# Unread products ahead of MLP1, strided products one place sooner, and one local tile behind the second score round, in a sparse-attention and MLP kernel

## The chip, the cores and the metric

The kernel runs on one core of a Trainium2 chip. The metric is the device time of one execution in microseconds (us), median of several. A profile is a look at one execution, and its span is some 1.8 us shorter than the device time of the same execution. TensorE does the matmuls, VectorE (DVE) and ScalarE (ACT) the elementwise work, GpSimd (POOL) casts and masks, and the SyncE queue (SPq) issues most transfers.

## The reference, cut to what matters

Eight batches of 576 tokens go through attention with eight heads. Four heads are local (a token sees the 32 last tokens), four strided (it sees earlier tokens of the same residue modulo 32). The result, 4608 x 512, goes through an MLP.

```python
x = attn_out.transpose(0, 2, 1, 3).reshape(B * S, H * D)   # 4608 x 512
h = x @ w_in                                               # 512 -> 2048   (MLP1)
g = h * np.tanh(np.log1p(np.exp(h)))
return g @ w_out                                           # 2048 -> 512   (MLP2)
```

## The kernel before: the parts that matter

The MLP works in nine blocks `t` of 512 tokens. The attention of batch `t + 1` is cut into steps that are issued between the groups of four matmuls of block `t`: `str_steps` (strided products with v, one step behind each item of MLP1) and `loc_steps` (local scores and products, and the next batch's strided scores, behind the items of MLP2). Scores go through ScalarE (exponential), a mask on VectorE or GpSimd, and the product with v on TensorE (`V`). VectorE then divides by the sums and transposes (`xt_str`). PSUM tiles of the products rotate over two buffers.

```python
def str_steps(b):
    ...
    return [
        [], [], [V(0)], [V(1)], [V(2)], [V(3)], [V(4)], [V(5)], [V(6)], [V(7), a.xt_str],
    ]

def loc_steps(b, x, y):
    ...
    return [
        [],
        [Q(x, ("l", 0)), Q(None, ("l", 2), *n2), Q(y, ("l", 1)), M("l", 0), M("l", 2)],
        [], [],
        [V(0), V(1), M("l", 1)],
        [V(5)] + ([Q(x, ("n", 0)), Q(y, ("n", 1))] + N) * more + [a.xt_str_copy],
        ...
```

Ahead of the first block, batch 0 is worked off alone, and TensorE waits often:

```python
a.pv2("l", 0, 1)
a.mask("l", 2, Dv)
a.pv2("l", 2, 0)
a.pv("l", 4)       # gap behind it: the mask of the last scores
a.pv("l", 5)       # gap behind it: VectorE's divisions
a.xt("l", 0)
a.xt("l", 1)
...                # then MLP1 of block 0
```

The softmax here doesn't subtract the row's maximum and nothing guards it: scores larger than these inputs give would overflow.

## Time and profile before

| | before |
|---|---|
| device time, first three runs | 314.27 us (314.21 to 314.87) |
| span of the profile | 312.8 us |
| TensorE busy | 94% |
| MLP1's first matmuls at half speed | 7 |
| stalls of TensorE at local products (near 150, 183, 213 us) | 0.57, 0.23, 0.25 us |

A stall here is the start of a group less the start of the group before it and the time of its matmuls (0.216 us for 512 columns). The profile's own bracket is shorter (0.40 us near 150 us, against 0.57), since the ends of matmuls in it are modelled. The lines stand in the prediction below.

### The profile page before, as it was taken

Reading aid. Unit: us, or ns where it says so; the run is one execution under the profiler, and the core shown is the slowest. Engines: PE = TensorE matmul, PEld = TensorE weight load, DVE = VectorE, ACT = ScalarE, POOL = GpSimd, SP = SyncE. Lnnn points to the kernel's source line nnn. Section 1 sums busy time; section 2 is a strip of 40 time slices with the busy share of each in tenths; the row PEclk is TensorE's granted clock in tenths of the full one; section 3 lists DMA queues with packets and bytes.
Section 4 is the critical chain, followed back from the end, with each engine's and each line's share of the span. In section 5 each row is a group of like instructions: output and inputs, shape, how many; then the busy total and the mean of one; then the engine's idle time right before and its main releaser. Section 6 shows DMA issues by size and latency. Waiting matters only on the chain.

```text
span 312.8 us, 5771 instructions
## 1 busy us (share of the span) xinstructions
PE 295.3 (94%) x2376; PEld 156.2 (50%) x2376; DVE 164.6 (53%) x378; ACT 182.6 (58%) x195; POOL 102.4 (33%) x109
## 2 busy tenths in 40 slices
PE   0687999999999999999999999999999999999995
PEld 0563455544454445554469754545454444444444
DVE  7673066700571048569786988698869870000000
ACT  1673653476647673867786778677767937215501
POOL 9199043263046105230791079108800000000000
PEclk9999999999999999999999999999999999999999
DMA  6999999999999999999987999898330030011011
GB/s 174 203 226 206 221 185 199 176 168 130 222 188 207 126 221 187 197 165 211 188 162 127 208 169 185 146 198 159 103 107 2 0 132 4 0 67 69 0 67 67
DMA packets 96985, 45.14 MB, mean 144 GB/s; under 512 B 79040, under 2 KB 89600, under 8 KB 96960
## 3 DMA queue, kind: packets, MB, share of 16 engines
q1 hardware_dynamic: 85520, 35.66, 61.8%
q0 software_dynamic: 11152, 8.92, 18.8%
q8 instruction: 18, 0.29, 0.4%
q10 hardware_dynamic: 288, 0.21, 0.2%
q14 instruction: 7, 0.06, 0.1%
HBM read 36.78 MB, written 9.44 MB: 148 GB/s over the span
## 4 chain that ended last, share of the span: by engine, by line
PE 85%; DVE 11%; ACT 2%; issue 1%; DVEq 0%
PE psh L507 38%; PE pso L530 31%; PE po L323 5%; PE pso L557 4%; PE ps L286 3%; DVE xs_t L397 3%; DVE Pl L307 2%; DVE ks L149 1%; DVE x_l L335 1%; PE trx L362 1%; PE tr L209 1%; DVE x_s L335 1%; PE trx L372 1%; DVE rden L334 1%; DVE Ps L601 0%
## 5 line engine op out<-in xcount | busy, mean ns | idle before, releaser
L507 PE MATMUL psh<-xT,w_in 128*128 128x512 bf16 (+1 forms) x640 | 131.9, 361 | 0.3 <-ACT Ps L299 0.3
L530 PE MATMUL pso<-w_out,gT 128*128 128x512 bf16 x512 | 121.8, 379 | 0.0
L513 ACT ACTIVATE gT<-psh 128x1024 bf16<-128x1024 f32 x72 | 72.4, 1023 | 50.1 <-PE psh L507 50.1
L507 PEld LDWEIGHTS <-w_in 128*128 128x128 bf16 x640 | 60.5, 98 | 57.1 <-issue 2.5
L530 PEld LDWEIGHTS <-gT 128*128 128x128 bf16 x512 | 45.4, 98 | 45.8
L149 POOL CAST kl<-kl 96x768 bf16<-96x768 f32 (+1 forms) x13 | 12.5, 984 | 78.8 <-DMA kl<-in_k_dram 78.8
L397 DVE STREAM_TRANSPOSE xs_t<-x_s 32x512 bf16<-32x512 bf16 x48 | 33.7, 702 | 0.9
L334 DVE RECIPROCAL rden<-po 72x4 f32<-72x4 f32 (+1 forms) x100 | 17.6, 176 | 28.1 <-PE po L323 27.2
L537 ACT COPY osb<-pso 128x1024 f32<-128x1024 f32 x16 | 17.6, 1100 | 24.3 <-PE pso L530 13.9
L307 DVE TENSOR_TENSOR Ps<-Ps,consts_sb 72x864 bf16<-72x864 bf16 (+3 forms) x15 | 10.2, 688 | 38.6 <-ACT Ps L299 38.6
L149 DVE COPY osb<-pso 128x512 f32<-128x512 f32 (+1 forms) x2 | 1.1, 558 | 51.3 <-PE pso L557 51.3
L388 DVE STREAM_TRANSPOSE xT<-x_l 32x384 bf16<-32x384 bf16 x48 | 27.3, 569 | 0.7
L149 POOL CAST vl<-vl 128x768 bf16<-128x768 f32 (+2 forms) x30 | 23.6, 785 | 9.0 <-DMA vl<-in_v_dram 7.6
L299 ACT ACTIVATE Ps<-ps 72x864 bf16<-72x864 f32 (+3 forms) x21 | 17.4, 860 | 13.4 <-PE ps L286 13.4
L335 DVE TENSOR_TENSOR x_s<-po,rden 72x256 bf16<-72x256 f32 x56 | 23.5, 420 | 1.9
L323 PEld LDWEIGHTS <-Ps 72*128 72x128 bf16 x256 | 15.5, 101 | 12.0 <-DVE Ps L307 0.8
L404 ACT COPY xT<-xs_t 128x576 bf16<-128x576 bf16 x8 | 21.4, 2938 | 0.0
L299 ACT ACTIVATE Pl<-ps 128x960 bf16<-128x960 f32 (+1 forms) x20 | 17.3, 874 | 3.7 <-PE ps L286 3.5
L335 DVE TENSOR_TENSOR x_l<-po,rden 96x256 bf16<-96x256 f32 x44 | 18.5, 421 | 1.5
L323 PE MATMUL po<-vs,Ps 72*128 72x65 bf16 x256 | 18.2, 201 | 0.7 <-DVE x_s L349 0.5
L147 ACT COPY xT<-trx 128x576 bf16<-128x576 bf16 x16 | 9.9, 636 | 14.7 <-PE trx L372 11.5
L149 POOL CAST ql<-ql 96x768 bf16<-96x768 f32 (+1 forms) x13 | 12.2, 965 | 8.7 <-DMA ql<-in_q_dram 8.7
(73 smaller groups left out, 224.3 us busy)
## 6 DMA issues: line engine op xcount, KB each, us to landing
out_dram<-osb SPq DMA_DIRECT2D x16, 512.0 KB, 4.9
vs<-in_v_dram SPq DMA_DIRECT2D x8, 576.0 KB
vl<-in_v_dram SPq DMA_DIRECT2D x8, 576.0 KB, 11.2
kl<-in_k_dram SPq DMA_DIRECT2D x7, 576.0 KB, 17.0
ql<-in_q_dram SPq DMA_DIRECT2D x7, 576.0 KB, 10.8
w_out<-in_moe_w_out_dram POOLq DMA_DIRECT2D x4, 512.0 KB, 14.2
ks<-in_k_dram POOLq DMA_DIRECT2D x7, 288.0 KB, 8.0
qs<-in_q_dram POOLq DMA_DIRECT2D x7, 288.0 KB, 8.8
```

What stands on the lines that cost most here:

```text
L149: eng.tensor_copy(out_, in_)
L299: nc.scalar.activation(pt[0:n, :, 0:nw], t[0:n, :, o0:o0 + nw], AF.Exp, scale=scale)
L323: nc.tensor.matmul(po[:, h, :], lhsT=pt[0:n, c0:c0 + 128], rhs=rhs, start=True, stop=True,)
L334: nc.vector.reciprocal(rden[0:m, :], po[0:m, :, D])
L335: nc.vector.tensor_tensor(out=dst.rearrange("p (h d) -> p h d", h=4), in0=po[0:m, :, 0:D], in1=rden[0:m, :].unsqueeze(2).to_broadcast([m, ...
L388: nc.vector.transpose(dst[32 * q:32 * q + 32, :, :, m:m + 32], src[m:m + 32, :, :, q, :])
L397: nc.vector.transpose(xs_t[32 * q:32 * q + 32, :, :, m:m + 32], src[m:m + 32, :, :, q, :])
L404: nc.scalar.copy(xT[:, 2 + c, t0:t0 + S].rearrange("p (n j) -> p j n", j=CS), xs_t[:, :, c, 0:PN])
L507: nc.tensor.matmul(ps[:, u, o:o + n], lhsT=w_in[:, cc, fc * 128:(fc + 1) * 128], rhs=xT[:, cc, a:a + n], start=(cc == 2 and o == 0), stop= ...
L513: nc.scalar.activation(gT[:, 2 * g:2 * g + 2, :], ps[:], AF.Mish)
L530: nc.tensor.matmul(p[:, ot % 2, :], lhsT=gT[:, fc, 128 * ot:128 * ot + 128], rhs=w_out[:, fc, :], start=(fc == 0), stop=(fc == 15),)
L537: nc.scalar.copy(osb[:], p[:])
```

## The change

Its intent: keep the array busy ahead of MLP1, so that its clock is already at full rate when MLP1 starts (26.55 us before); and let VectorE begin its transposes of the strided outputs sooner, so that the masks of the local scores no longer wait behind them.

```diff
-            [], [], [V(0)], [V(1)], [V(2)], [V(3)], [V(4)], [V(5)], [V(6)], [V(7), a.xt_str],
+            [], [V(0)], [V(1)], [V(2)], [V(3)], [V(4)], [V(5)], [V(6)], [V(7), a.xt_str],
...
-            [V(5)] + ([Q(x, ("n", 0)), Q(y, ("n", 1))] + N) * more + [a.xt_str_copy],
+            ([Q(x, ("n", 0)), Q(y, ("n", 1))] + N) * more + [a.xt_str_copy, V(5)],
...
+    def fill(t, *widths):
+        for w in widths:
+            nc.tensor.matmul(t[:, 0:w], lhsT=ident, rhs=kTs[0][:, 0:w], start=True, stop=True)
...
         a.pv("l", 4)
+        fill(acc(2, "fill")[:, 0, :], 512, 256)
         a.pv("l", 5)
+        fill(acc(2, "fill")[:, 0, :], 512, 512)
```

## The prediction

It puts the fill at 23.55 to 24.19 and 24.45 to 25.30 us: 0.64 us for 768 columns and 0.85 us for 1024. That is an estimate, and the slow matmuls of MLP1 bear it out: their weight loads from 26.97 to 29.53 us stand 0.427 us apart, for 512 columns each.

> **What bounds the kernel now.** I read the page first (who is busy, what the chain of work is made of), then the chain in order of time, then the TensorE timeline at the places where the chain left TensorE, then the timelines of VectorE and the weight loads there. The page:
>
> ```profile
> PE 295.3 (94%) x2376; PEld 156.2 (50%) x2376; DVE 164.6 (53%) x378; ACT 182.6 (58%) x195; POOL 102.4 (33%) x109
> PE 85%; DVE 11%; ACT 2%; issue 1%; DVEq 0%
> ```
>
> TensorE sets the time. [...] VectorE's 11% of the chain counts only where TensorE stood still for it. So I looked for stalls of TensorE, and for matmuls slower than they can be.
>
> First place, the start of MLP1 (TensorE timeline, then weight loads):
>
> ```profile
> 22.25 1.29 PE L323 MATMUL po<-vl,Pl 128*128 128x65 bf16 x20
> 24.16 0.40 PE L323 MATMUL po<-vl,Pl 128*128 128x65 bf16 x4 [0.63 <-DVE Pl L307]
> 25.55 1.21 PE L362 MATMUL trx<-consts_sb,x_l 96*128 96x96 bf16 x12 [0.98 <-DVE x_l L335]
> 26.55 5.75 PE L507 MATMUL psh<-xT,w_in 128*128 128x512 bf16 x19
> ```
>
> ```profile
> 28.68 0.15 PEld L507 LDWEIGHTS <-w_in 128*128 128x128 bf16 x1 [0.28 <-issue]
> 29.11 0.15 PEld L507 LDWEIGHTS <-w_in 128*128 128x128 bf16 x1 [0.28 <-issue]
> 29.53 2.48 PEld L507 LDWEIGHTS <-w_in 128*128 128x128 bf16 x12 [0.28 <-issue]
> ```
>
> Two gaps, of 0.63 and 0.98 us, stand right ahead of MLP1. Then MLP1's weight loads come singly every 0.43 us until 29.53 us, and from there twelve in 2.48 us, 0.21 us each. Later a block of 64 such matmuls takes 13.81 us in the chain, 0.216 us each. So seven matmuls of MLP1 (26.55 to 29.53) ran at half speed. The page's row of granted clock shows full speed in that slice: it doesn't show this, the spacing does.
>
> Second place, the second products in the blocks where scores, masks and products interleave with MLP2 (TensorE, then VectorE, then the chain one block later):
>
> ```profile
> 147.41 2.76 PE L530 MATMUL pso<-w_out,gT 128*128 128x512 bf16 x12
> 150.57 0.43 PE L323 MATMUL po<-vl,Pl 128*128 128x65 bf16 x8 [0.40 <-DVE Pl L307]
> ```
>
> ```profile
> 140.59 8.58 DVE L397 STREAM_TRANSPOSE xs_t<-x_s 32x512 bf16<-32x512 bf16 x12
> 149.20 1.58 DVE L307 TENSOR_TENSOR Pl<-Pl,consts_sb 128x960 bf16<-128x960 bf16 x2
> ```
>
> ```profile
> 180.79 1.55 DVE Pl L307 x2
> 182.34 0.10 DVE rden L334
> ...
> 182.47 0.43 DVE x_l L335
> 182.90 0.05 issue
> 182.94 0.30 PE po L323 x4
> ```
>
> The twelve matmuls from 147.41 are through at 147.41 + 12 x 0.216 = 150.00; the local products start at 150.57. They wait for the mask of the local scores, which stood behind the twelve transposes of the strided outputs on VectorE (140.59 to 149.17).
>
> [...]
>
> **The change part by part.**
>
> *Unread products.* Added: matmuls of 512 and 256 columns in the first gap, 512 and 512 in the second. [...] The first gap opens when the twentieth product ends: the group starts at 22.25, 20 x 0.065 = 1.30, so 23.55. Filled to 24.19, where the next product starts at 24.16 now: 0.03 us late, and nobody feels it, since VectorE is busy until 24.95 with the tiles before. The four products take 0.26, so the second fill lies from 24.45 to 25.30, and the transposes start at 25.55. The fill thus costs the path nothing; no operand of it arrives late, and the accumulator it writes was read last at 22.5.
> What it may save: seven matmuls x (427 - 216) = 1.48 us, and if the array is warm before 25.55, perhaps 0.2 us more in the twelve transposes. [...] I take 60% for the full saving of 1.5 us, 25% for about a third of it, 15% for none: 0.9 + 0.13 = about 1.0 us.
>
> *Strided products one place sooner.* The eight groups of products come behind items 1 to 8 of MLP1 in place of 2 to 9. They are 0.99 us apart, so VectorE starts its transposes 0.99 us sooner and ends at 148.2 instead of 149.17. The mask then needs ScalarE's exponentials, ready at 147.44 + 0.97 = 148.41. It moves from 149.20 to about 148.45, 0.75 us sooner. It took 1.32 us here beside a GpSimd cast (0.65 elsewhere), so it ends by 149.8, ahead of TensorE's 150.00. Stall of this block gone: 150.57 - 150.00 = 0.57. In the block at 212 us the twelve matmuls from 210.09 end at 212.68 and the products start at 212.94: 0.25 us; the mask there moves from 211.94 to about 211.15, enough. The block at 244 us has no such stall.
>
> *One local tile behind the second score round.* Its stall is in the block at 183 us: TensorE was ready at 182.72 (products 181.59, 0.27 for eight, 0.86 for four matmuls) and began at 182.94 when VectorE had emptied the first of the two rotating PSUM tiles: 0.23 us. Now 28 score matmuls (0.56 us) come before it, and the masks come 0.75 us sooner. Either suffices. It also lets the scores start 0.13 us sooner; ScalarE isn't bound there.
>
> Sum of the stalls: 0.57 + 0.25 + 0.23 = 1.05 us, all on TensorE's path. The counts of work stay as they were, but for the four added matmuls. With the fill: 1.05 + 1.0 = about 2.1 us.
>
> **The rivals.**
> 1. *The fill does not release the clock.* [...] Its failure would leave 1.05 us: 313.2.
> 2. *The clock comes early, but a transfer takes the place of the wait.* The transposes by DMA of the strided queries, issued at 67.39, land 9.6 us later at 77.0; their first readers run at 78.9. That queue runs on its own loads, so a TensorE 1.5 to 1.7 us ahead arrives at 77.2 to 77.4, with 0.2 us left. It would eat at most some tenths: 312.3. Against it: it still fits. The weights fit: the small copy that waits for the last part of w_in is issued at 32.77, and that part is first read after 48 matmuls, at 26.55 + 48 x 0.216 = 36.9.
> 3. *VectorE becomes the wait at the start of the strided products.* In the block at 161 us its transposes of local outputs end at 163.31, and the first strided product will now want VectorE at 163.46 instead of 164.46. That leaves 0.15 us; a miss would delay VectorE only, which then has 0.36 us idle per product to catch up. Worth zero, and up to 0.1 us if not. GpSimd's cast of v for that block ended at 162.24, before its first reader at 163.13.
> 4. *The stalls come back later*, at MLP1's accumulators, which ScalarE frees (161.71 to 162.72 for the second). ScalarE's work follows TensorE's, so both move together; I see no new wait.
>
> **Range and chances.** 314.27 - 2.1 = 312.2, and I take 312.1 us, since warm transposes may add a little. With all of the clock gain, 311.4; with none, 313.2; runs scatter by 0.3 to 0.6. The range is 311.2 to 313.4. Two per cent would be 6.3 us, three times all I can find: faster 0.01, same 0.98, slower 0.01.
>
> **What would show it.** Right: MLP1's first weight loads 0.21 us apart from the start; no single ones at 0.43 us. The local products start where the twelve MLP2 matmuls end, in all four blocks. The masks start at the end of the exponentials. Wrong: singles at 0.43 us for 3 us after the fill; a TensorE wait on a transfer near 77 us; the first gap's products later than 24.3 us; or stalls at the local products left.

## The result, and the profile after

| | before | changed |
|---|---|---|
| device time, median of six runs | 314.81 us (314.21 to 316.19) | 312.70 us (312.04 to 313.23) |
| ratio of fast runs | | 0.9924 (0.9897 to 0.9951) |
| span of the profile | 312.8 us | 311.5 us |

A ratio is the mean time of one kernel's fast runs over that of the other's in the same rounds, so it isn't quite the ratio of the medians. The change is worth 0.76%, 2.4 us.

The changed kernel's TensorE timeline at the start of MLP1 (start, duration, what, times, and in brackets the idle time before it and what ended it):

```profile
22.53 1.29 PE L323 MATMUL po<-vl,Pl 128*128 128x65 bf16 x20
24.05 0.42 PE L489 MATMUL fill<-kTs,consts_sb 128*128 128x256 bf16 x1 [0.22 <-issue]
24.45 0.40 PE L323 MATMUL po<-vl,Pl 128*128 128x65 bf16 x4
24.66 0.78 PE L489 MATMUL fill<-kTs,consts_sb 128*128 128x512 bf16 x2
25.83 0.98 PE L362 MATMUL trx<-consts_sb,x_l 96*128 96x96 bf16 x12 [0.39 <-DVE x_l L335]
26.65 7.72 PE L512 MATMUL psh<-xT,w_in 128*128 128x512 bf16 x34
```

and its weight loads there:

```profile
26.38 0.28 PEld L362 LDWEIGHTS <-x_l 96*128 96x128 bf16 x6 [0.28 <-DVE x_l L335]
26.61 7.48 PEld L512 LDWEIGHTS <-w_in 128*128 128x128 bf16 x36
```

The reader is to see 36 weight loads in 7.48 us, 0.21 us each, from the very first: no single loads 0.43 us apart are left. (One record of the first gap's fill is missing from the trace, as some are: it has 2342 matmuls and 2380 weight loads.) The trace records when the granted clock rose: 25.04 us here, 29.54 us before.

The local products, same places as before (TensorE, then VectorE):

```profile
147.02 2.76 PE L535 MATMUL pso<-w_out,gT 128*128 128x512 bf16 x11
149.62 0.42 PE L323 MATMUL po<-vl,Pl 128*128 128x65 bf16 x8
```

```profile
139.34 8.57 DVE L397 STREAM_TRANSPOSE xs_t<-x_s 32x512 bf16<-32x512 bf16 x12
148.06 0.93 DVE L307 TENSOR_TENSOR Pl<-Pl,consts_sb 128x960 bf16<-128x960 bf16 x2
```

The twelve matmuls (eleven on record) from 147.02 are through at 149.61, and the products start at 149.62. The masks end at 148.99, 0.63 us ahead of that. The stalls near 183 and 213 us are gone too (nothing over 0.12 us is left there). So the parts did what they were meant to. But the span fell by 1.3 us only, where 1.5 us at the clock and 1.05 us at the stalls make 2.5. The rest is in two waits that the kernel before did not have. The first, on the TensorE timeline and then on the queue that serves it:

```profile
75.92 1.89 PE L535 MATMUL pso<-w_out,gT 128*128 128x512 bf16 x8
78.70 0.57 PE L286 MATMUL ps<-qTs,kTs 64*128 64x72 bf16 x24 [0.89 <-DMA qTs<-qs]
```

```profile
60.36 8.81 SPq L170 DMA_TRANSPOSE kTs<-ks  x1
69.27 5.98 SPq L170 DMA_TRANSPOSE qTs<-qs  x1
```

The strided queries of batch 2 are transposed by a transfer that was issued at 69.27 here (67.39 before) and landed 9.3 us later. Before, TensorE came at 78.93 and found them. Now it was ready at 77.65, and stood for 1.05 us. The second is in the block near 162 us: 0.17 us ahead of the first strided product. Both are looked at below.

### The profile page after: what moved, and what is told of

Its sections match the earlier page's. It is cut to its first block, busy times and chain, and to the rows that moved or that the text cites.

```text
span 311.5 us, 5741 instructions
## 1 busy us (share of the span) xinstructions
PE 291.6 (94%) x2342; PEld 155.9 (50%) x2380; DVE 162.8 (52%) x378; ACT 182.7 (59%) x195; POOL 102.0 (33%) x109
## 4 chain that ended last, share of the span: by engine, by line
PE 71%; DMA 16%; SPq 7%; DVE 2%; POOL 2%; issue 1%; ACT 0%; POOLq 0%
PE psh L512 30%; PE pso L535 29%; DMA vl<-in_v_dram 9%; PE pso L562 4%; DMA w_in<-in_moe_w_in_dram 4%; PE po L323 4%; DMA qTs<-qs 3%; SPq L170 3%; SPq L120 3%; PE ps L286 3%; POOL vl L149 2%; DVE x_l L335 1%; DVE x_s L335 1%; SPq L581 0%; DVE rden L334 0%
## 5 line engine op out<-in xcount | busy, mean ns | idle before, releaser
L512 PE MATMUL psh<-xT,w_in 128*128 128x512 bf16 (+1 forms) x629 | 129.4, 357 | 0.8 <-ACT Ps L299 0.3
L535 PE MATMUL pso<-w_out,gT 128*128 128x512 bf16 x487 | 117.7, 379 | 1.9 <-issue 0.6
L307 DVE TENSOR_TENSOR Ps<-Ps,consts_sb 72x864 bf16<-72x864 bf16 (+3 forms) x15 | 8.3, 556 | 40.9 <-ACT Ps L299 40.9
L149 POOL CAST ql<-ql 96x768 bf16<-96x768 f32 (+1 forms) x13 | 11.4, 903 | 11.5 <-DMA ql<-in_q_dram 11.5
```

What stands on the lines that cost most here:

```text
L149: eng.tensor_copy(out_, in_)
L512: nc.tensor.matmul(ps[:, u, o:o + n], lhsT=w_in[:, cc, fc * 128:(fc + 1) * 128], rhs=xT[:, cc, a:a + n], start=(cc == 2 and o == 0), stop= ...
L535: nc.tensor.matmul(p[:, ot % 2, :], lhsT=gT[:, fc, 128 * ot:128 * ot + 128], rhs=w_out[:, fc, :], start=(fc == 0), stop=(fc == 15),)
```

## The experiments

Twelve kernels ran, four to a chip, each beside the kernel before on the same chip. Ratios are to the kernel before of the same call; the three calls were on three chips, so absolute times are compared within a call only. The profiled execution is the first of each kernel's runs, and not always a typical one: it was the slowest of the changed kernel's six, of e1's seven, e2's six, e6's five and e11's eighteen. A wait that its profile shows need not be in the median.

**What each profile showed.** The columns: when the clock rose; how many of MLP1's weight loads were spaced 0.43 us and not 0.21; the stall at the queries of batch 2; and the stall ahead of the first strided product of the block near 162 us (in us, only those over 0.12, from the starts of matmuls). "First look" is the changed kernel's profile in the result above; e6 is the second look at the same kernel.

| run | fill | clock rose | half speed | queries | first strided product | span |
|---|---|---|---|---|---|---|
| before | none | 29.54 | 7 | | | 312.8 |
| changed, first look | full | 25.04 | 0 | 1.05 | 0.17 | 311.5 |
| e1, fill only (slow) | full | 25.02 | 0 | 3.71 | | 316.4 |
| e2, moves only | none | 28.64 | 5 | 1.45 | 1.33 | 313.8 |
| e3, strided move only | none | 30.05 | 8 | | | 312.0 |
| e4, late v (wrong) | full | 26.73 | 0 | | | 310.6 |
| e5, late v, mended | full | 26.58 | 0 | | | 310.9 |
| e6, changed again | full | 27.86 | 3 | | 0.48 | 311.3 |
| e7, v cast first | full | 27.00 | 1 | | | 310.2 |
| e8, both mends | full | 25.09 | 0 | | | 310.2 |
| e9, half-height fill | half | 30.47 | 9 | | | 312.1 |
| e10, fill of transposes | full | 25.09 | 0 | | 1.63 | 312.1 |
| e11, second gap only | part | 28.35 | 4 | | 1.93 | 314.3 |
| e12, moves, v cast first | none | 32.01 | 12 | | | 312.7 |

### The parts apart: e1, e2, e3

e1 undoes both moves and keeps the fill. e2 takes the two `fill` lines out. e3 is e2 with the local tile put back:

```diff
-            ([Q(x, ("n", 0)), Q(y, ("n", 1))] + N) * more + [a.xt_str_copy, V(5)],
+            [V(5)] + ([Q(x, ("n", 0)), Q(y, ("n", 1))] + N) * more + [a.xt_str_copy],
```

> Only the unread products; strided and local products where they were before. Theory T1 (the fill releases the clock some 4 us sooner, but TensorE then meets the queries' transfer for batch 2, which lands at about 77 to 78.6 us whatever TensorE does): MLP1 is at full speed from its first weight load, a TensorE wait of 0.3 to 1 us on the queries' transfer stands near 77 us, the three stalls near 150, 183 and 213 us stay, and the time falls by only 0.4 to 1.0 us. Rival R1 (the fill's 1.5 us come out in full): falls by 1.4 to 1.6 us. Rival R2 (the fill gives nothing): within 0.2 us of before.

Measured: 313.36 us against 315.16, ratio 0.9937 (0.9915 to 0.996): 2.0 us less (1.3 to 2.7). That is above the 0.4 to 1.0 us of T1; R1's 1.4 to 1.6 us lie inside the interval. The clock rose at 25.02, as in the changed kernel. The profiled execution was of the slow state, so it is left out of every ratio, but its trace says itself what happened to it (stretch and its length, then the busy time of PE, PEld, DVE, ACT and POOL with their counts of instructions, granted clock, share of the DMA engines, GB/s):

```profile
74.00:77.00 3.00, 3.00 (x16) 1.30 (x14) 0.00 (x0) 2.28 (x3) 0.00 (x0) 1.00 1.56 122
77.00:80.00 3.00, 0.33 (x2) 0.00 (x0) 0.00 (x0) 0.96 (x1) 0.00 (x0) 0.94 1.27 131
80.00:83.00 3.00, 1.79 (x27) 1.23 (x29) 0.60 (x1) 1.55 (x2) 0.00 (x0) 0.50 0.78 153
83.00:86.00 3.00, 3.00 (x16) 1.35 (x15) 1.01 (x3) 0.12 (x1) 0.00 (x0) 0.50 0.95 300
```

TensorE came 3.71 us ahead of the queries' transfer, and the clock fell again: at 79.63, for 6.83 us. Nothing more is concluded from that execution.

> Only the two moves, no unread products. T1: the three stalls of 0.57, 0.23 and 0.25 us vanish, the time falls by about 1.05 us (0.8 to 1.3); MLP1 starts with six to a dozen matmuls at half speed. Rival (stalls come back as others, at the accumulators or behind ScalarE): falls by less than 0.6 us.

Measured: 314.12 us, 0.9975 (0.9948 to 1.0001): 0.8 us less, with an interval from none to 1.6. MLP1 started with five slow matmuls (six to a dozen were expected). All three stalls at the local products were gone in the profile. But it had two new ones: 1.45 us at the queries, with no fill and so no early TensorE (the transfer was simply late in that execution, the slowest of the six), and this (TensorE, then GpSimd):

```profile
161.77 1.91 PE L512 MATMUL psh<-xT,w_in 128*128 128x256 bf16 x16
164.84 0.28 PE L323 MATMUL po<-vs,Ps 72*128 72x65 bf16 x4 [1.17 <-POOL vs L149]
```

```profile
155.05 1.60 POOL L149 CAST ql<-ql 96x768 bf16<-96x768 f32 x2 [2.63 <-DMA ql<-in_q_dram]
156.60 0.72 POOL L102 DMA_DIRECT2D ks<-in_k_dram  x1
157.31 0.71 POOL L102 DMA_DIRECT2D qs<-in_q_dram  x1
158.11 4.85 POOL L307 TENSOR_TENSOR Ps<-Ps,consts_sb 72x1008 bf16<-72x1008 bf16 x3
162.91 1.88 POOL L149 CAST vs<-vs 72x2048 bf16<-72x2048 f32 x1
```

The strided products, now behind the second item of MLP1, read v in bf16, which GpSimd casts last in a queue that starts when q has landed. With q cast from 155.05 (151.72 before), the cast ended at 164.79, and the product waited for it.

> Only the strided products one place sooner. If either move suffices for the stall near 183 us, as the prediction said, the time equals that of both moves (1.05 us below before, within 0.15) and no stall of over 0.1 us is left at the local products. Rival: the local tile's move is needed, a stall of about 0.2 us stays near 183 us and the time is 0.2 to 0.3 us above that of both moves.

Measured: 313.79 us, 0.9959 (0.994 to 0.9978): 1.3 us less. No stall of over 0.1 us at the local products, near 183 us too (the eight products start at 181.33, four matmuls, the fifth tile at 182.45 without a wait). So the local tile's move was not needed once the strided products came sooner; either move would do, as predicted, though the local move alone was not run. That e2 seems slower than e3 is within the two intervals.

### The two waits: e4 to e8

e4 puts the load of batch 2's local v behind that batch's transposes in the same queue; e5 is its mended form; e7 lets GpSimd cast the strided v ahead of the masks; e8 has both; e6 is the changed kernel itself.

```diff
 # e5
-            load_v(2)
+            load_v_str(2)
...
-            cast_v(2, Po, Po)
+            cast(Po, vs[0][0:PN, :, :, 0:D], vs32[0:PN])
...
-                at[9] += [lambda: str_by_dma(2), lambda: loc_by_dma(2)]
+                at[9] += [
+                    lambda: str_by_dma(2), lambda: loc_by_dma(2),
+                    lambda: load_v_loc(2), lambda: cast_v_loc(2, Po),
+                ]
 # e7
-                    at[5].append(lambda: cast_v(t + 2, Po, Po))
+                    at[5].insert(2, lambda: cast(
+                        Po, vs[t % 2][0:PN, :, :, 0:D], vs32[0:PN]
+                    ))
+                    at[5].append(lambda: cast_v_loc(t + 2, Po))
```

> The changed kernel, with the load of the local v of batch 2 (576 KB) behind the transposes by DMA of batch 2 in the same queue, not ahead of them. T1: the queries' transfer lands 2 to 3 us sooner, TensorE no longer waits near 77 us, and the time falls by a further 0.5 to 1.0 us below the changed kernel, to about 2.3 to 2.6 us below before in all. Rival (the wait near 77 us is a chance of one execution): no difference to the changed kernel, 2.0 to 2.2 us below before.

Its result was wrong (relative error 0.20): the cast of the local v stayed ahead of the moved load and took the old batch's values. Its time is not used.

> The run with the late load of v, mended: its cast of the local v moves behind the load too (the first try cast the old batch's v and gave a wrong result). T1: no TensorE wait on the queries' transfer near 78 us, 0.3 to 1.0 us faster than the changed kernel of the same rounds. Rival: equal to the changed kernel within 0.15 us.

> The changed kernel again, in the same rounds as its variants. T1: the clock rises before MLP1's first weight load; a wait of 0.3 to 1.5 us on the queries' transfer near 78 us; the first strided product of the block near 162 us waits 0 to 1.3 us for GpSimd's cast of v; about 312.5 us, 2 us below before. Rival: a profile without these two waits and the same time, so that they cost nothing in most executions.

> The changed kernel, with GpSimd casting the strided v ahead of the masks of the next block's strided scores, not behind them, in the three blocks that do it there. T2 (the strided products, one place sooner, now meet that cast): the cast ends 2 to 3 us before its first reader, no wait on it is left near 162 us, and the time is 0.1 to 0.6 us below the changed kernel. Rival (the wait of the run with the moves only was a chance): equal within 0.15 us; or slower, if v lands later than the cast is now wanted and holds up the masks.

> Both mends: late load of the local v of batch 2, and the strided v cast first. T1 and T2: the gains add; TensorE has no wait of over 0.35 us after MLP1's start but the one for an accumulator near 130 us and the small ones of the second and third block; 0.5 to 1.4 us below the changed kernel, some 311.5 us. Rival: a further transfer takes over and the time stays within 0.3 us of the better single mend.

| run | median | ratio to before (315.46) | 95% interval |
|---|---|---|---|
| e6, changed | 312.35 us | 0.9906 | 0.9889 to 0.9923 |
| e5, late v | 312.74 us | 0.9908 | 0.9889 to 0.9927 |
| e7, v cast first | 312.19 us | 0.9916 | 0.9877 to 0.9956 |
| e8, both | 312.51 us | 0.9905 | 0.9887 to 0.9922 |

(e7's runs hold one of 316.38 among five from 311.82 to 312.39.) In the profiles the mends did what they were to do. In e5 the queries' transfer was issued early:

```profile
58.63 2.65 SPq L170 DMA_TRANSPOSE kTs<-ks  x1
61.34 4.33 SPq L170 DMA_TRANSPOSE qTs<-qs  x1
```

eight microseconds sooner than in the changed kernel's first look, six sooner than in its second, and TensorE found them. In e7 the cast ran from 154.36, and its first reader came at 161.18:

```profile
154.36 1.89 POOL L149 CAST vs<-vs 72x2048 bf16<-72x2048 f32 x1 [0.25 <-DMA vs<-in_v_dram]
156.29 4.83 POOL L307 TENSOR_TENSOR Ps<-Ps,consts_sb 72x1008 bf16<-72x1008 bf16 x3
```

But none of it shows in the times: the four ratios lie between 0.9905 and 0.9916, and I had expected 0.5 to 1.4 us of e8. The intervals would still allow some 0.8 us between e8 and e6. The changed kernel's second look tells why at least in part. On this chip the queries were there in time, with no fix at all, and the wait for the cast was 0.48 us:

```profile
160.08 1.91 PE L512 MATMUL psh<-xT,w_in 128*128 128x256 bf16 x16
162.31 0.28 PE L323 MATMUL po<-vs,Ps 72*128 72x65 bf16 x4 [0.32 <-POOL vs L149]
```

(That look also missed an expectation: the clock rose at 27.86, after MLP1's first loads, and three matmuls ran at half speed.) And the late load of v brought a wait of its own, which e8's expectation of no new wait over 0.35 us missed. GpSimd could cast the local v only from 82.24, and TensorE stood 0.45 us for it (TensorE, then GpSimd):

```profile
86.26 0.29 PE L323 MATMUL po<-vl,Pl 128*128 128x65 bf16 x4 [0.29 <-POOL vl L149]
```

```profile
82.24 3.97 POOL L149 CAST vl<-vl 128x768 bf16<-128x768 f32 x4 [11.75 <-DMA vl<-in_v_dram]
```

In e5 a stall of 0.30 us stands at the same products, with no cause named by its profile; the kernels without the late load have none there.

So the two waits are real where they occur, and hang on when the transfers land in that execution. The eleven looks at kernels that share this queue's order had the queries issued at 67.39 to 69.27 us; in the two looks at the changed kernel it was 69.27 and 67.60. No version is shown to beat the changed kernel.

### What releases the clock: e9 to e12

e9 gives the fill 64 rows in place of 128, e10 makes it of transposes, e11 leaves out the first gap's fill, and e12 is e2 with e7's edit.

```diff
 # e9
-            nc.tensor.matmul(t[:, 0:w], lhsT=ident, rhs=kTs[0][:, 0:w], start=True, stop=True)
+            nc.tensor.matmul(t[:, 0:w], lhsT=ident[0:64, :], rhs=kTs[0][0:64, 0:w], start=True, stop=True)
 # e10
+            for c in range(0, w, 128):
+                nc.tensor.transpose(t.bitcast(BF16)[:, c:c + 128], kTs[0][:, c:c + 128], ident)
 # e11
-        fill(acc(2, "fill")[:, 0, :], 512, 256)
```

> The changed kernel, with unread products of the same widths and times over 64 rows of the array in place of 128. If the clock's release counts the array's rows (the half-height score products ahead of it never released it), the fill counts half: the clock rises at 28 us or later, MLP1 starts at half speed as in the kernel before, and the time is 1 to 2 us above the changed kernel. Rival (it counts time under any product): the clock rises between 25 and 28 us as with the full fill, and the time is that of the changed kernel, some 3 us below before.

Measured: 313.62 us against 315.25, 0.9949 (0.9929 to 0.9968). The fill took the same time, and MLP1 started slow (TensorE, then weight loads):

```profile
23.48 0.82 PE L489 MATMUL fill<-kTs,consts_sb 64*128 64x512 bf16 x2
24.56 1.03 PE L489 MATMUL fill<-kTs,consts_sb 64*128 64x512 bf16 x2
```

```profile
29.97 0.15 PEld L512 LDWEIGHTS <-w_in 128*128 128x128 bf16 x1 [0.28 <-issue]
30.39 2.52 PEld L512 LDWEIGHTS <-w_in 128*128 128x128 bf16 x12 [0.28 <-issue]
```

The clock rose at 30.47, with nine matmuls at half speed: as without a fill (5 to 12), not as with the full one (0 to 3). In the traces the full clock lasted 283.31 us seven times, 286.72 us five times and 279.89 us once (e1 apart, where it fell in between), so a rise, counted back from the fall of its execution, may come sooner or later by steps of some 3.41 us, an estimate from these three lengths. One such step earlier is 30.47 - 3.41 = 27.06, where it did not rise with 64 rows, and in e7 it rose at 27.00 with 128. The two lie within 0.06 us of each other, so it is most likely the height that made the difference. It is one pair of executions, on two chips. (In the kernel before, too, score products over 64 rows ran between 11.21 and 20.91 us, and the clock rose at 29.54.)

> The changed kernel, with the fill as TensorE transposes of 128 by 128 (four for each 512 columns), the same columns in about the same time. [...] as without a fill, the clock rises at 28 to 32 us, 1.5 to 2.5 us above the changed kernel. Rival (they count as products do): as the changed kernel.

Measured: 314.02 us, 0.9962 (0.9933 to 0.9992). Here the first expectation fell. The clock rose at 25.09, at the same moment as with products in e8 (25.09), and MLP1 ran at full speed at once:

```profile
23.35 0.83 PE L490 MATMUL fill<-consts_sb,kTs 128*128 128x128 bf16 x6
24.38 0.94 PE L490 MATMUL fill<-consts_sb,kTs 128*128 128x128 bf16 x8
```

So transposes of 128 by 128, 14 on record from 23.35 us on, did here what products did. (The trace names them MATMUL.) The time is no witness here: this profile lost 1.63 us to GpSimd's cast (e2's lost 1.33) and 0.83 us to another transfer of queries, and the changed kernel was not run on this chip.

> The changed kernel without the fill of the first gap (768 of 1792 columns left out). [...] the clock rises 0 to 3 us later, 0.3 to 1 us above the changed kernel in the median. Rival (the second gap is enough): no difference.

Measured: 313.91 us in 18 runs, 0.9954 (0.9938 to 0.997). The clock rose at 28.35, four matmuls late. One step of 3.41 us (the estimate above) earlier is 24.94, where it did not rise; in the changed kernel's first look, with both fills, it rose at nearly the same place, 25.04. So the first gap's fill most likely mattered there, by one execution each. How much fill is enough was not shown: e6, with both fills, rose at 27.86 only. The 18 runs spread from 312.44 to 316.08. The profile, of the slowest of them, shows 1.93 us of waiting for the cast and 0.84 us for a transfer of queries near 126 us, so this time too holds more than the fill.

> Both moves without the fill, with GpSimd's cast of the strided v ahead of the masks. T2: the wait on that cast that the run with the moves only showed (1.2 us near 163 us) is gone, the moves give their 1.05 us: 0.9967 of before. Rival: the same 0.9975 as the moves only, because that wait was a chance of one execution.

Measured: 313.99 us, 0.9964 (0.9944 to 0.9983): 1.1 us less, beside 0.8 for e2. The profile had no wait for the cast, on a chip where e10 and e11 had 1.63 and 1.93 us. That agrees with the mend working where the cast is late, but e9, on the same chip and without the mend, had no such wait either, the intervals of e2 and e12 overlap widely, and the chips differ. So the rival, a chance of one execution, is not excluded. It also shows the latest rise of the clock in any look: 32.01 us, twelve matmuls at half speed.

The times of these four kernels (ratios 0.9949 to 0.9964) don't tell them apart, though the clock rose at 25.09 in one and at 32.01 in another. What releases the clock is read from the traces alone.

## Why the prediction was right

312.1 us in 311.2 to 313.4 was predicted, and 312.70 measured; within 2%, as said. By its steps:

- *TensorE sets the time, its stalls and its slow matmuls are what counts.* Right.
- *The fill costs the path nothing.* Right: the products behind the first gap start at 24.16 or 24.17 in e6, e7 and e8, 24.16 in the kernel before (the first look's 24.45 is an execution that ran 0.28 us late from before the fill), and the transposes at 25.53 to 25.55 (25.55 before). One reading was off, without harm: the twenty products start 0.055 us apart, not 0.065, so the gap opened at 23.35, where e10's fill starts, and the fill had more room than reckoned.
- *What the fill saves: 1.0 us, as a chance of 60% for 1.5.* Undersized. With the full fill of products, seven looks show 0, 0, 0, 0, 3, 1 and 0 half-speed matmuls; without one, four show 7, 5, 8 and 12. The means are 0.6 and 8, and 7.4 x 0.21 us = 1.6 us; the fill by itself measured 2.0 (1.3 to 2.7). The term was 1.0 us mainly because the prediction left 40% for a fill that does little (rival 1, which did not come true), and a little because it took the seven of one execution for the usual cost, where four looks show 5 to 12. In all seven looks the clock had risen by 27.86 us; in the four without it rose at 28.64 to 32.01. (The twelve transposes ahead of MLP1 also got shorter in the first look: 0.82 us from their start to MLP1's, 1.00 before.) But the prediction's sign of being right, no single load at 0.43 us, holds in five of the seven only.
- *The moves remove 1.05 us.* The stalls went as worked out, all three. What reached the end was 0.8 us (e2), 1.3 (e3) and 1.1 (e12), each with 0.6 to 0.8 us to either side, which neither confirms nor refutes the size.
- *Rival 2, a transfer takes the place of the wait, at most some tenths.* It came true in the first look, 1.05 us, and with it a sign that the prediction had named as showing it wrong, a wait on a transfer near 77 us. The step that failed is "with 0.2 us left": it took the landing of one execution (77.0) as fixed, and in the next it was at 78.6 (69.27 + 9.3). In the second look at the same kernel it did not occur.
- *Rival 3, worth zero; "GpSimd's cast of v for that block ended at 162.24, before its first reader at 163.13".* This step failed. (The rival's own point, VectorE as the wait, did not come: no look shows TensorE waiting for VectorE there.) It moved the reader by its own 0.99 us and forgot that the fill and the removed stalls move TensorE as a whole, while the cast is tied to transfers. The first look had them meet (0.17 us), the second 0.48, and others up to 1.9 us.

- *Rival 4, stalls that come back at MLP1's accumulators.* As predicted, it did not come: the first look shows no new wait there.

So the sum came out for a mixed reason, and partly by luck: the clock gave more than reckoned, and waits on transfers and on the cast took some back in single executions. How much they take in the median stays open, since the two mends that remove them did not show in the times.

## What to carry to other kernels

Where TensorE idles briefly ahead of a dense stretch, as here (0.63 and 0.98 us), look whether that stretch starts at half speed: here 5 to 12 matmuls took 0.43 us in place of 0.216. Look at the spacing of the weight loads, not at the page's clock row (it showed 9 in every slice while seven matmuls ran at 0.43 us), and try to fill the gaps with full-height work that nobody reads: 0 to 3 slow matmuls were left with it, nine with half the height. When a change moves the bounding engine forward, list every operand that is tied to transfers and not to that engine, and subtract the whole advance, not just the moved instruction's own. Look at a second and third execution before one profile's slack, or one profile's count of slow matmuls, is used as a constant.
